# Two small DMAs issued by ScalarE instead of SyncE, and two more Relu blocks by halves

## The chip, the cores and the metric

The kernel runs on one core of a Trainium2 chip. The metric is device time in microseconds (us) of one execution, as the median of several runs. A lower number is better.

The core's engines each work through their own list of instructions in order and wait for each other on counting semaphores: TensorE (PE) multiplies matrices, VectorE (DVE) and ScalarE (ACT) do elementwise work and read PSUM, GpSimd (POOL) does elementwise work in SBUF, and SyncE (SP) issues most DMAs. Any of ACT, POOL and SP can issue a DMA; the transfer itself then runs on the core's 16 DMA engines.

## What is computed

A causal depthwise convolution of 7 taps over 4096 tokens, for 8 sequences of 192 channels, whose taps are the softmax of a weight for each of 8 heads. On its result, a feed-forward layer with 1536 hidden channels:

```python
w = exp(weight - max) ; w = w / (sum + 1e-09)          # 8 heads x 7 taps
x = einsum('hk,bskhg->bshg', w, x_unfolded)            # 8 x 4096 x 192
gate = maximum(x @ w_gate, 0.0)                        # 32768 x 1536
val  = x @ w_val
out  = (gate * val) @ w_out                            # 32768 x 192
```

## The kernel before

The tokens are worked in 16 units. A unit is 1024 tokens of one sequence and the same 1024 tokens of the sequence four further on; these two are the two **streams** (`st` 0 and 1). One stream lies on partitions 0 to 63 and the other on 64 to 127, and the 192 channels are three groups (`c` 0, 1, 2, "thirds") of 64. So the convolved input of unit 0 is the tile `xc[0]`, of 128 partitions, three thirds and 1024 tokens. A unit has two windows (`w`) of 512 tokens.

`gate_val(u, w)` makes the hidden layer of one window in 12 blocks (`f` 0 to 11, "first" to "twelfth") of 128 hidden channels. For one block PE runs six matmuls for gate and six for val (L600). ACT takes the Relu of gate from PSUM into `gr` (L611), and DVE multiplies it with val into `hT` (L612). Gate and val of a block have a PSUM buffer each, of four in turn, so the gate of block f+2 can't be begun before the Relu of block f is over, and its val not before DVE's product of block f. In four blocks of the first window (first, second, fifth, sixth) Relu and product are made by streams: two halves of 128x512, so that DVE can begin when the first half is there. The others are one instruction of 128x1024 each.

The start is arranged by hand. Unit 0's first 512 tokens are convolved by PE (`first_block`), and the window begins. The second 512 tokens are convolved by PE before the fifth block (`second_block`). Part of its result comes out on other partitions than it belongs: it is evicted to `held` (in the tile `out_s`, L433) and brought to its place by eight DMAs from SBUF to SBUF (L438): 40 partitions of the first third, 8 and 8 of the second, 40 of the last, each for both streams. SP issues all eight. The second window, `gate_val(0, 1)`, reads them: its first six gate matmuls go through the thirds in order, both streams each.

Behind the moves, SP issues nine DMA transposes (L885), which bring the input of unit 1 into channel layout (`x_r` from `x_p`). They need POOL's copies into `x_p` (L517). Ahead of the moves SP issues ten DMAs of a few hundred bytes that spread the taps (L854).

The DMAs of SP and ACT count on **eight semaphores, DMAHW0 to DMAHW7**. Each DMA adds 16 to one of them when it has landed, and before it is issued the issuing engine waits until the DMA that used that semaphore before has landed. The framework that builds the program hands them out in turn, one after the other, in the order in which its own plan of the program places the DMAs, over both engines together.

Beyond unit 0 everything repeats: 24 blocks of gate and val, then the projection with `Wo`, with the convolution of the units to come on ACT, DVE and POOL beside it.

Of the kernel before, what the change touches and what calls it, by code (L numbers as in the profile page):

```python
# [18 lines left out]
def kernel(  # L19
# [12 lines left out]
    nc = tc.nc  # L32
# [81 lines left out]
    def stage(p0, rows, st, n_st, jj, n):  # L114
        at = room[p0 : p0 + rows, 0, 0, 0:1]
        dims = [[D * GSUB, n_st], [D, n], [1, D]]
        return bass.AP(
            tensor=at.tensor,
            offset=at.offset + D * (GSUB * st + jj),
            ap=[at.ap[0]] + [d for d in dims if d[1] > 1],  # L120
        )
# [3 lines left out]
    def body(st):  # L125
# [8 lines left out]
        out=stage(PAD, FIRST, 0, 2, 0, 1),  # L134
        in_=bass.AP(
            tensor=x.tensor, offset=x.offset, ap=[[D, FIRST], [NB * S * D, 2], [1, D]]
        ),
# [111 lines left out]
    def bits(src, n, down, keep):  # L249
# [13 lines left out]
        out=mx[:], in_=wr[:], axis=mybir.AxisListType.X, op=ALU.max, negate=True  # L263
# [6 lines left out]
    with nc.allow_low_precision("zero and one"):  # L270
        nc.vector.tensor_tensor(
            out=same[:], in0=col[:, 0:SEG], in1=s_of[:].to_broadcast([SUB, SEG]), op=ALU.is_equal
# [12 lines left out]
    with nc.allow_low_precision("zero and one"):  # L285
        nc.vector.tensor_scalar(
            out=places[:, SUB - SEG : SUB - SEG + NROW],
# [7 lines left out]
        out=spread[0:SUB, 0, 0:H],  # L295
# [7 lines left out]
    with nc.allow_low_precision("products with one and zero"):  # L303
        nc.vector.tensor_tensor(
            out=diag[:],
# [6 lines left out]
    for a in range(2):  # L312
        for b in range(NSEG):
            nc.tensor.matmul(
                out=(bps, spread)[a][:, a, HB * SEG * b : HB * SEG * (b + 1)],
# [9 lines left out]
    for c in range(NCH):  # L325
        cols = slice(64 * c, 64 * c + 64)
        nc.scalar.copy(
            out=xts[0][0:ROWS0, 1:GSUB, 0, cols],
            in_=stage(0, ROWS0, 0, 1, 1, GSUB - 1)[:, :, cols],
# [28 lines left out]
    xc = {}  # L358
# [40 lines left out]
    def conv_heads(g, ps, bank, slots):  # L399


        xt = xts[g]
        toks = GROUPS[g][1]
        t0 = toks[0]
        ends = toks[1:] + [t0 + WIN]
        for jj in range(GSUB):
            col, n = toks[jj] - t0, ends[jj] - toks[jj]
            rows = n + PAD
            for i, (st, ch, h) in enumerate(slots):
                nc.tensor.matmul(  # L410
                    out=ps[32 * i : 32 * i + 32, bank, col : col + n],
                    lhsT=xt[0:rows, jj, st, ch : ch + 32],
                    rhs=band(h)[0:rows, 0:n],
                    start=True,
                    stop=True,
                    tile_position=(0, 32 * i),
                    skip_group_check=True,
                )
# [3 lines left out]
    def second_block():  # L422
        aside, inplace = [psum.tile([128, 2, 512], FP, name="ps") for _ in range(2)]
        conv_heads(1, aside, 0, [(0, ch, h) for ch, h in ASIDE])
        conv_heads(1, inplace, 0, [(st, ch, h) for st in range(2) for ch, h in ((0, 0), (160, 7))])
        conv_heads(1, inplace, 1, [(st, ch, h) for st in range(2) for ch, h in ((64, 3), (96, 4))])
        conv_heads(1, aside, 1, [(1, ch, h) for ch, h in ASIDE])
        late = slice(WIN, 2 * WIN)
        os_ = opool.tile([128, 4, D], FP, name="out_s")
        flat = os_[:].rearrange("p a d -> p (a d)").bitcast(F16)  # L430
        held = flat[:, 0 : 2 * WIN].rearrange("p (s t) -> p s t", s=2)
        nc.scalar.copy(out=xc[0][:, 0, late], in_=inplace[:, 0, :])
        nc.scalar.copy(out=held, in_=aside[:])  # L433
        nc.vector.tensor_copy(out=xc[0][:, 1, late], in_=inplace[:, 1, :])
        nc.vector.tensor_copy(out=xc[0][:, 2, late], in_=inplace[:, 0, :])
        for c, r, p0, n in ((0, 24, 8, 40), (1, 0, 48, 8), (1, 56, 72, 8), (2, 0, 80, 40)):
            for st in range(2):
                nc.sync.dma_start(  # L438
                    out=xc[0][64 * st + r : 64 * st + r + n, c, late],
                    in_=held[p0 : p0 + n, st, :],  # L440
                )

    HEADS = (((0, 1), (3, 4)), ((6, 7), (2, 5)))

# [140 lines left out]
    def gate_val(u, w):  # L585
        h = hpool.tile([128, NFF, 2, WIN], F16, name="hT")
        xcb = xc[u]
        for f in range(NFF):
            if u == 0 and w == 0 and f == 4:
                second_block()  # L590
            pss = [psum.tile([128, 2, 512], FP, name="ps") for _ in range(2)]
            order = [(i, c) for i in range(2) for c in range(NCH)]
            if u == 0 and w == 0 and f == 0:
                order = [(i, c) for c in range(NCH) for i in range(2)]
            M = 64 if 0 < u < NUNIT - 1 else 128
            for i, c in order:
                W = (Wg, Wv)[i]
                for st in range(2):
                    for m in range(0, 128, M):
                        nc.tensor.matmul(  # L600
                            out=pss[i][m : m + M, st, :],
                            lhsT=W[64 * st : 64 * st + 64, c, 128 * f + m : 128 * f + m + M],
                            rhs=xcb[64 * st : 64 * st + 64, c, WIN * w : WIN * (w + 1)],
                            start=(c == 0),
                            stop=(c == NCH - 1),
                            tile_position=(64 * st, m),
                        )
            by_stream = u == 0 and w == 0 and f in (0, 1, 4, 5)
            for sts in (slice(0, 1), slice(1, 2)) if by_stream else (slice(0, 2),):
                gr = gpool.tile([128, 2, WIN], F16, name="gr")  # L610
                nc.scalar.activation(out=gr[:, sts], in_=pss[0][:, sts], func=ACTF.Relu)  # L611
                nc.vector.tensor_tensor(  # L612
                    out=h[:, f, sts], in0=gr[:, sts], in1=pss[1][:, sts], op=ALU.mult
                )
        return h

    def slots():
# [232 lines left out]
    for h in range(H):  # L850
        r = G * h
        while r < G * (h + 1):
            c, n = r // 64, min(64 - r % 64, G * (h + 1) - r)
            nc.sync.dma_start(  # L854
                out=tap[r % 64 : r % 64 + n, c, :],
                in_=taps[h : h + 1, :].unsqueeze(1).to_broadcast([1, n, KW]),
# [18 lines left out]
    for u in range(NUNIT):  # L875
# [6 lines left out]
        if u == 0:  # L882
            hs.append(gate_val(0, 0))
            for go in turns:
                go()  # L885
# [23 lines left out]
        while len(hs) < 2:  # L909
            hs.append(gate_val(u, len(hs)))  # L910
# [50 lines left out]
```

## Time and profile before

| | us |
|---|---|
| median of 3 runs | 761.53 (761.35 to 761.76) |
| time of the profiled execution | 762.13 |
| its span in the trace | 760.4 |
| PE busy | 756.0 (99%) |
| DVE busy | 708.4 (93%) |
| ACT busy | 618.4 (81%) |
| POOL busy | 404.2 (53%) |

Times in the trace count from the start of the span. "SPq" and "ACTq" are the parts of SP and ACT that issue DMAs; the length of such a row is that of the issuing instruction, and the transfer lands later. In brackets at the end of a row stands how long the engine was idle before and what ended it. A page's shares are means over the whole span; this change touches a stretch of some 20 us at its start, so the rows of that stretch matter most.

### The profile page before, as it was taken

To read this page: it belongs to the slowest core of one execution; us is meant where nothing else is said; L and a number is where in the kernel's file an instruction comes from. 1 tells how busy PE (TensorE), PEld (TensorE's weight loads), DVE (VectorE), ACT (ScalarE), POOL (GpSimd) and SP (SyncE) were. 2 spreads that over 40 slices of the span, in tenths; PEclk is the share of its full clock that TensorE was granted. 3 is DMA by queue.
4 is the path that set the end of the run, shared out by engine and by line. 5 is a ranking of instruction groups with operands and counts; after the bars stand their busy time and mean duration, and the time that the engine had idled before them with its cause. 6 is when DMAs were issued, how large, how long until landed. Compare 5 with 4: busy or idle time off the path is not lost.

```text
span 760.4 us, 30579 instructions
## 1 busy us (share of the span) xinstructions
PE 756.0 (99%) x13597; PEld 484.5 (64%) x13597; DVE 708.4 (93%) x771; ACT 618.4 (81%) x725; POOL 404.2 (53%) x262
## 2 busy tenths in 40 slices
PE   9999999999999999999999999999999999999998
PEld 5595555555666666666666666666666666666548
DVE  7998999999999999999999999999999999999891
ACT  7787887978879798898988979788797887976672
POOL 9519549094490935819267291763908549091000
PEclk9999999999999999999999999999999999999999
DMA  9969229589396983949749597594966939544732
GB/s 135 129 106 134 24 64 176 140 98 195 91 183 151 87 184 98 206 119 119 171 93 180 134 147 172 80 183 112 173 145 101 178 109 139 158 113 110 187 85 84
DMA packets 231700, 100.61 MB, mean 132 GB/s; under 512 B 185296, under 2 KB 220816, under 8 KB 231568
## 3 DMA queue, kind: packets, MB, share of 16 engines
q1 hardware_dynamic: 190528, 83.12, 53.3%
q0 software_dynamic: 40896, 15.50, 19.9%
q8 instruction: 106, 1.74, 1.0%
q14 instruction: 26, 0.21, 0.1%
q10 hardware_dynamic: 144, 0.03, 0.0%
HBM read 31.48 MB, written 47.19 MB: 103 GB/s over the span
## 4 chain that ended last, share of the span: by engine, by line
PE 96%; DMA 2%; SPq 1%; ACT 0%; issue 0%; POOLq 0%
PE ps L600 63%; PE ps L713 29%; PE ps L629 3%; PE ps L680 1%; DMA tap<-taps 1%; SPq L854 1%; DMA xc<-out_s 1%; DMA x_h<-in_x_dram 1%; SPq L438 0%; ACT xc L397 0%; PE ps L456 0%; PE ps L379 0%; ACT acc L688 0%; ACT taps L848 0%; POOLq L945 0%
## 5 line engine op out<-in xcount | busy, mean ns | idle before, releaser
L612 DVE TENSOR_TENSOR hT<-gr,ps 128x1024 f16<-128x1024 f16 (+1 forms) x388 | 469.1, 1210 | 29.9 <-ACT gr L611 3.4
L611 ACT ACTIVATE gr<-ps 128x1024 f16<-128x1024 f32 (+1 forms) x388 | 393.3, 1015 | 100.8 <-PE ps L600 100.7
L548 POOL TENSOR_TENSOR prods<-prods 128x1344 f32<-128x1344 f32 x70 | 213.0, 3042 | 268.8 <-DVE prods L544 265.5
L600 PE MATMUL ps<-xc,Wg 64*64 64x512 f16 (+1 forms) x4320 | 322.6, 376 | 0.5 <-DMA xc<-out_s 0.5
L600 PE MATMUL ps<-xc,Wv 64*64 64x512 f16 (+1 forms) x4320 | 322.2, 376 | 0.0
L713 PE MATMUL ps<-hT,Wo 64*64 64x512 f16 x4032 | 220.2, 376 | 0.0
L600 PEld LDWEIGHTS <-Wg 64*64 64x64 f16 (+1 forms) x4320 | 155.4, 106 | 93.6 <-issue 0.6
L600 PEld LDWEIGHTS <-Wv 64*64 64x64 f16 (+1 forms) x4320 | 153.0, 105 | 96.3 <-issue 1.8
L713 PEld LDWEIGHTS <-Wo 64*64 64x64 f16 x4032 | 139.7, 107 | 77.8
L572 DVE SCALAR_TENSOR_TENSOR acc<-x_r,tap,acc 128x576 f32<-128x576 f16 x225 | 165.3, 813 | 0.0
L542 ACT ACTIVATE prods<-x_r,tap 128x448 f32<-128x448 f16 x222 | 127.2, 659 | 0.0
L735 ACT COPY x_h<-ps 128x2048 uint16<-128x2048 uint16 x28 | 51.8, 1848 | 8.8 <-PE ps L713 8.8
L215 POOL DMA_DIRECT2D x_e<-in_x_dram x58 | 46.9, 818 | 12.8 <-ACT acc L558 12.5
L517 POOL COPY x_p<-x_e 128x960 f16<-128x960 f16 (+1 forms) x58 | 50.4, 914 | 1.0 <-DMA x_e<-in_x_dram 0.9
L548 POOL TENSOR_TENSOR xc<-prods 128x1344 f16<-128x1344 f32 x14 | 42.5, 3038 | 1.1
L735 POOL COPY y<-x_h 128x2048 uint16<-128x2048 uint16 x14 | 26.6, 1898 | 23.3 <-ACT x_h L791 23.3
L572 DVE SCALAR_TENSOR_TENSOR xc<-x_r,tap,acc 128x576 f16<-128x576 f16 x45 | 34.1, 813 | 0.0
L558 ACT ACTIVATE acc<-x_r,tap 128x576 f32<-128x576 f16 x45 | 31.4, 765 | 0.0
L544 DVE TENSOR_SCALAR prods<-x_r,tap 128x448 f32<-128x448 f16 x70 | 27.7, 449 | 0.0
L629 PE MATMUL ps<-Wo,hT 64*128 64x192 f16 x576 | 24.6, 243 | 0.0
L629 PEld LDWEIGHTS <-hT 64*128 64x128 f16 x576 | 24.0, 94 | 0.4
L791 ACT COPY x_h<-ps 128x512 f32<-128x512 f32 x14 | 8.2, 587 | 10.9 <-ACT x_h L735 6.3
(69 smaller groups left out, 92.4 us busy)
## 6 DMA issues: line engine op xcount, KB each, us to landing
out_dram<-out_s SPq DMA_DIRECT2D x62, 384.0 KB
held<-x_h SPq DMA_DIRECT2D x14, 512.0 KB
held<-x_h SPq DMA_DIRECT2D x28, 256.0 KB
held<-y SPq DMA_DIRECT2D x14, 512.0 KB
x_e<-in_x_dram POOLq DMA_DIRECT2D x34, 192.0 KB, 6.7
x_e<-in_x_dram POOLq DMA_DIRECT2D x24, 240.0 KB, 5.3
x_r<-x_p SPq DMA_TRANSPOSE x131
out_s<-held SPq DMA_TRANSPOSE x56
```

What stands on the lines that cost most here:

```text
L215: first = nc.gpsimd.dma_start(out=xe[:, j0 + start : j0 + n, st, :, :].rearrange("p j c r -> p j (c r)"), in_=bass.AP(tensor=x.tensor, off ...
L517: nc.gpsimd.tensor_copy(out=xp[:, j0 : j0 + n, :, st, :], in_=xe[:, j0 : j0 + n, st, :, :])
L542: engine.activation(out=out, in_=in_, func=ACTF.Copy, scale=scale)
L548: nc.gpsimd.tensor_tensor(out=pr[:, 0] if k < KW - 1 else xc[v + 1][:, :, LDVE:UNIT], in0=pr[:, 0], in1=pr[:, k], op=ALU.add,)
L558: nc.scalar.activation(out=accs[v][:, c, :], in_=shifted(v, c, 0, 0), func=ACTF.Copy, scale=tap[:, c, 0:1],)
L572: nc.vector.scalar_tensor_tensor(out=xc[v][:, c, 0:LDVE] if k == KW - 1 else acc[:, c, :], in0=shifted(v, c, k, 0), scalar=tap[:, c, k : k ...
L600: nc.tensor.matmul(out=pss[i][m : m + M, st, :], lhsT=W[64 * st : 64 * st + 64, c, 128 * f + m : 128 * f + m + M], rhs=xcb[64 * st : 64 * ...
L611: nc.scalar.activation(out=gr[:, sts], in_=pss[0][:, sts], func=ACTF.Relu)
L612: nc.vector.tensor_tensor(out=h[:, f, sts], in0=gr[:, sts], in1=pss[1][:, sts], op=ALU.mult)
L629: mm = nc.tensor.matmul(out=outs[q], lhsT=h[64 * r : 64 * r + 64, f, st, 128 * q : 128 * (q + 1)], rhs=Wo[64 * r : 64 * r + 64, f, :], sta ...
L713: mm = nc.tensor.matmul(out=ps[bank][64 * half : 64 * half + 64], lhsT=Wo[64 * r : 64 * r + 64, f, d : d + 64], rhs=hs[w][64 * r : 64 * r ...
L735: copy(out=pt[:], in_=src[:].bitcast(U16).rearrange("p b (t l) -> p b l t", l=2))
```

## The change

The two moves of the last third (40 partitions, 512 tokens, one for each stream) are taken from SP's list. ACT issues them: the one for stream 0 behind the Relu of the sixth block (`f == 5`), that for stream 1 behind the Relu of the eighth (`f == 7`). The seventh and the ninth block (`f` 6 and 8), which follow them on ACT, are made by streams. Bytes, places and the other six moves stay.

```diff
-        for c, r, p0, n in ((0, 24, 8, 40), (1, 0, 48, 8), (1, 56, 72, 8), (2, 0, 80, 40)):
+
+        def move(queue, st, c, r, p0, n):
+            queue.dma_start(
+                out=xc[0][64 * st + r : 64 * st + r + n, c, late],
+                in_=held[p0 : p0 + n, st, :],
+            )
+
+        for piece in ((0, 24, 8, 40), (1, 0, 48, 8), (1, 56, 72, 8)):
             for st in range(2):
-                nc.sync.dma_start(
-                    out=xc[0][64 * st + r : 64 * st + r + n, c, late],
-                    in_=held[p0 : p0 + n, st, :],
-                )
+                move(nc.sync, st, *piece)
+        return [partial(move, nc.scalar, st, 2, 0, 80, 40) for st in range(2)]
@@ gate_val
             if u == 0 and w == 0 and f == 4:
-                second_block()
+                moves = second_block()
...
-            by_stream = u == 0 and w == 0 and f in (0, 1, 4, 5)
+            by_stream = u == 0 and w == 0 and f in (0, 1, 4, 5, 6, 8)
...
+            if u == 0 and w == 0 and f in (5, 7):
+                moves.pop(0)()
```

In the program that is built, this is ACT's order from the evictions of the second block on, before (`gr` is the Relu's output; the last number is the tile's shape; in brackets the semaphores that are waited for):

```order
L432 CAST xc<-ps 128x512 [waits PE_49]
L433 CAST out_s<-ps 128x1024 [waits PE_49]
L611 ACTIVATE gr<-ps 128x512 [waits DVE_49,PE_49]
L611 ACTIVATE gr<-ps 128x512 [waits DVE_49]
L611 ACTIVATE gr<-ps 128x512 [waits DVE_49,PE_49]
L611 ACTIVATE gr<-ps 128x512 [waits DVE_49]
L611 ACTIVATE gr<-ps 128x1024 [waits DVE_49,PE_49] x18
```

and with the change:

```order
L616 ACTIVATE gr<-ps 128x512 [waits DVE_49,PE_49]
L616 ACTIVATE gr<-ps 128x512 [waits DVE_49]
L438 DMA xc<-out_s 40x512 [waits DMAHW6_49]
L616 ACTIVATE gr<-ps 128x512 [waits DVE_49,PE_49]
L616 ACTIVATE gr<-ps 128x512 [waits DVE_49]
L616 ACTIVATE gr<-ps 128x1024 [waits DVE_49,PE_49]
L438 DMA xc<-out_s 40x512 [waits DMAHW5_49]
L616 ACTIVATE gr<-ps 128x512 [waits DVE_49,PE_49]
L616 ACTIVATE gr<-ps 128x512 [waits DVE_49]
L616 ACTIVATE gr<-ps 128x1024 [waits DVE_49,PE_49] x15
```

Two DMA issues now stand between Relus, and each waits for a DMA semaphore, DMAHW6 and DMAHW5.

On SP the same stretch, from the first move on, was before:

```order
L438 DMA xc<-out_s 40x512 [waits DMAHW5_49,Activation_49]
L438 DMA xc<-out_s 40x512 [waits DMAHW6_49]
L438 DMA xc<-out_s 8x512 [waits DMAHW7_49,DVE_49]
L438 DMA xc<-out_s 8x512 [waits DMAHW0_49]
L438 DMA xc<-out_s 8x512 [waits DMAHW1_49]
L438 DMA xc<-out_s 8x512 [waits DMAHW2_49]
L438 DMA xc<-out_s 40x512 [waits DMAHW3_49,DVE_49]
L438 DMA xc<-out_s 40x512 [waits DMAHW4_49]
L885 DMA_TRANSPOSE x_r<-x_p 128x3x128 [waits DMAHW5_49,Pool_49]
L885 DMA_TRANSPOSE x_r<-x_p 128x3x128 [waits DMAHW6_49]
L885 DMA_TRANSPOSE x_r<-x_p 128x3x128 [waits DMAHW7_49]
```

and with the change, from the last of the six moves that are left:

```order
L438 DMA xc<-out_s 8x512 [waits DMAHW2_49]
L892 DMA_TRANSPOSE x_r<-x_p 128x3x128 [waits DMAHW3_49,Pool_49]
L892 DMA_TRANSPOSE x_r<-x_p 128x3x128 [waits DMAHW4_49]
L892 DMA_TRANSPOSE x_r<-x_p 128x3x128 [waits DMAHW5_49]
L892 DMA_TRANSPOSE x_r<-x_p 128x3x128 [waits DMAHW7_49]
L892 DMA_TRANSPOSE x_r<-x_p 128x3x128 [waits DMAHW0_49]
L892 DMA_TRANSPOSE x_r<-x_p 128x3x128 [waits DMAHW1_49,Pool_49]
L892 DMA_TRANSPOSE x_r<-x_p 128x3x128 [waits DMAHW2_49]
L892 DMA_TRANSPOSE x_r<-x_p 128x3x128 [waits DMAHW3_49]
L892 DMA_TRANSPOSE x_r<-x_p 128x3x128 [waits DMAHW4_49]
L663 DMA out_dram<-out_s 128x4x192 [waits PE_49,DMAHW6_49,Activation_49]
```

The semaphores run on in turn, but with two gaps: DMAHW6 between the third and the fourth transpose, and DMAHW5 between the ninth and the first output. These two went to ACT's moves. The counts in the built program say the same: ACT's first move waits until DMAHW6 stands at 32 (a tap DMA and the move of the first third for stream 1), its second until DMAHW5 stands at 48 (a tap DMA, the move of the first third for stream 0, and the third transpose).

## The prediction

> **What bounds the kernel now.** I read the page first, for the engine that sets the end:
>
> ```profile
> span 760.4 us, 30579 instructions
> PE 756.0 (99%) x13597; PEld 484.5 (64%) x13597; DVE 708.4 (93%) x771; ACT 618.4 (81%) x725; POOL 404.2 (53%) x262
> PE 96%; DMA 2%; SPq 1%; ACT 0%; issue 0%; POOLq 0%
> ```
>
> PE is busy for 99% of the span and makes 96% of the chain that ended last. Whatever makes PE wait is paid in full, since nothing later has slack to give it back; whatever spares PE a wait is earned in full. So only PE's waits in the stretch of the change count. The chain in order of time and PE's timeline there:
>
> ```profile
> 20.89 4.88 DMA xc<-out_s
> 25.81 4.19 PE ps L600 x36
> ...
> 21.95 0.83 PE L600 MATMUL ps<-xc,Wg 64*128 64x512 f16 x6
> 22.60 0.83 PE L600 MATMUL ps<-xc,Wv 64*128 64x512 f16 x6
> 23.25 0.83 PE L600 MATMUL ps<-xc,Wg 64*128 64x512 f16 x6
> 23.90 0.83 PE L600 MATMUL ps<-xc,Wv 64*128 64x512 f16 x6
> 24.54 0.81 PE L600 MATMUL ps<-xc,Wg 64*128 64x512 f16 x5
> 25.81 0.37 PE L600 MATMUL ps<-xc,Wg 64*128 64x512 f16 x1 [0.46 <-DMA xc<-out_s]
> ```
>
> Six matmuls start every 0.648 us (24.54 − 21.95 is four times that). The sixth of the second window's first gate should start 0.43 us after 24.54, with its pair, at 24.97; it starts at 25.81. It waited 0.84 us for the last of SP's eight moves, issued at 20.89 and landed at 25.77. This is what there is to win: 0.84 us, 0.11% of the span.
>
> **What is removed and moved.** SP gives up two issues of 0.7 us; behind them on SP stand only the transposes, which wait for POOL's copies until 24.1, so that saves nothing. If ACT's copy of the last move were issued right behind the eighth Relu, at about 20.2, it would land by 25.1 (the same 4.88 us), and 0.7 us of the 0.84 would be won. Whether it can be issued then is the question.
>
> **The waits that come with it.** Both moves now stand in ACT's own list, between Relus, and each waits for a DMA semaphore. Behind the first stand the Relus from the seventh block on, behind the second those from the ninth on; DVE's products wait for the Relus, and PE for both, two blocks later.
>
> The first waits until SP's second move (first third, stream 1) has landed. Its issue row, and the one tap DMA whose landing the chain shows:
>
> ```profile
> 16.25 0.73 SPq L438 DMA_DIRECT2D xc<-out_s  x1
> ...
> 13.10 6.27 DMA tap<-taps
> ...
> Wv<-in_moe_w_val_dram POOLq DMA_DIRECT2D x1, 48.0 KB, 3.4
> ```
>
> With the 4.88 us of the last move it lands at about 21.1; the 6.27 of the tap would make it 22.5, and the shortest landing of this stretch, 3.4 of a load of like size, 19.7. ACT has been ready since 17.43:
>
> ```profile
> 15.32 2.11 ACT L611 ACTIVATE gr<-ps 128x512 f16<-128x512 f32 x4
> 17.64 1.02 ACT L611 ACTIVATE gr<-ps 128x1024 f16<-128x1024 f32 x1 [0.21 <-PE ps L600]
> 18.93 1.02 ACT L611 ACTIVATE gr<-ps 128x1024 f16<-128x1024 f32 x1 [0.27 <-PE ps L600]
> 20.23 1.02 ACT L611 ACTIVATE gr<-ps 128x1024 f16<-128x1024 f32 x1 [0.27 <-PE ps L600]
> ```
>
> So the seventh Relu slips from 17.64 to about 21.6, and PE, out of buffers after the eighth block's val at 19.36, stands about 3.3 us (to 21.1 + 0.5 for the issue + two half Relus of 0.53). With the old wait gone this alone would be a net loss of 1.5 to 4 us.
>
> The second waits until DMAHW5 stands at 48: a tap, SP's first move, and **the third transpose**, which SP issues only after POOL's copies. SP's queue there:
>
> ```profile
> 24.15 1.31 SPq L885 DMA_TRANSPOSE x_r<-x_p  x1
> 25.52 1.65 SPq L885 DMA_TRANSPOSE x_r<-x_p  x1
> 27.20 1.87 SPq L885 DMA_TRANSPOSE x_r<-x_p  x1
> ```
>
> Its issue ends at 29.07. Nothing in the change makes it earlier: the first transpose starts when POOL has ended its second copy, POOL waits for nobody on ACT or PE there, and SP was idle before it:
>
> ```profile
> 22.21 1.91 POOL L517 COPY x_p<-x_e 128x960 f16<-128x960 f16 x2
> 24.07 1.02 POOL L869 DMA_DIRECT2D Wo<-in_moe_w_out_dram  x1
> 28.21 1.50 POOL L97 DMA_DIRECT2D x_h<-in_x_dram  x2 [0.32 <-issue]
> ```
>
> When does it land? No row gives a transpose's landing, but the DMA view gives what SP's queue (q1) moved, here from 24.15 to 33, to 34.8 and to 39.2:
>
> ```profile
> q1 hardware_dynamic: 1061, 0.26, 54.6%
> ...
> q1 hardware_dynamic: 1356, 0.33, 50.3%
> ...
> q1 hardware_dynamic: 3723, 0.89, 70.1%
> Wo<-in_moe_w_out_dram POOLq DMA_DIRECT2D x1, 576.0 KB, 9.2
> x_h<-in_x_dram POOLq DMA_DIRECT2D x2, 192.0 KB, 9.5
> ```
>
> 0.89 MB is nine transposes, so three are 0.30 MB. They are through not before some 33.7 (on the line from 0.26 MB at 33 to 0.33 MB at 34.8), and that only if the fourth and fifth, issued by then, have not yet moved a byte. The queue crawls because POOL's 576 KB of `Wo`, issued at 24.07, take 9.2 us of the same engines, to 33.3, and the `x_h` loads follow. I take 34.7, with 33.7 and 36 as ends. Until then ACT stands, and the ninth Relu is held back from 20.23 to behind it.
>
> **What it costs PE.** PE needs the ninth Relu's buffer for the eleventh block's gate, which began at 21.95. Now:
>
> 34.7, when the third transpose lands. Plus ACT's issue: ACT's one DMA in this trace took 0.37, SP's moves around 0.73:
>
> ```profile
> 757.91 0.37 ACTq L691 DMA_DIRECT2D out_dram<-acc  x1
> ```
>
> I take 0.5, as POOL issues nothing at that time. Plus the two halves of the ninth Relu, 2 × 0.53 (2.11 for four). That gives 36.3 for the eleventh gate instead of 21.95: **+14.3**. PE has stood for some 10 us by then, since the tenth block, the last for which it had buffers, is over by about 26.
>
> Then PE's speed after the stand. The nearest rows are its start, also after idling, and the 0.84 us wait, after which it went on at the old rate:
>
> ```profile
> 0.78 3.04 PE L161 MATMUL ps<-const-bfloat16-1.0 128*128 128x512 bf16 x7 [0.78 <-PEq L945]
> 3.96 0.61 PE L161 MATMUL ps<-const-bfloat16-1.0 128*128 128x512 bf16 x1
> 4.85 0.49 PE L161 MATMUL ps<-const-bfloat16-1.0 128*128 128x512 bf16 x2
> ```
>
> At the start seven matmuls of 512 columns took 3.04 us, 0.43 each, where the pair of L600 takes 0.216; at 3.96 a single one still took 0.61, against 0.37 at 25.81; at 4.85 two took 0.49 together. So for 3.8 us from its first matmul PE ran at half rate. (The granted clock of that stretch is given as 1.00 all the same.) An idle stretch of 10 us is nearer to that start than to 0.84 us: I take half rate for 3.8 us, **+1.9**. At the other end, full rate, a smaller loss stands in its place: DVE's product of the ninth block, two halves of 0.62 behind the two Relu halves, ends at 37.0, and PE would wait for it 0.3 us between gate and val of the eleventh block:
>
> ```profile
> 15.97 2.48 DVE L612 TENSOR_TENSOR hT<-gr,ps 128x512 f16<-128x512 f16 x4
> ```
>
> At half rate the gate itself lasts to 37.6, and DVE is hidden. The Trainium skill (TensorE: Matmul & The Clock Gate, Part 1) says that PE falls back to half clock after an idle window of about 3.4 us and needs about 3.4 us of sustained work to leave it; by its figure the term would be an estimated +1.7, and its cold gap for 512 columns, 427 ns, agrees with the 0.43 here.
>
> Less the old wait: the second move, issued at 34.7, lands at 39.6 (4.88) to 41.0 (6.27); PE needs it at 36.3 + 1.9 + 3.0 = 41.2 (four half blocks of 0.648 and 0.43). So that wait is gone: **−0.84**.
>
> Sum: 14.3 + 1.9 − 0.84 = **+15.4 us**. The seventh and ninth block by streams change little: four halves take DVE 2.48 and ACT 2.11 against 2.44 and 2.04 for two whole ones, beside ACT's stand. All that comes behind, transposes, loads and unit 1, was ready before it was needed and is so more than ever; PE does not catch up at 99%. On the profiled execution's span that is 775.8; on the median of the runs, which lies 1.1 above that span, 761.53 + 15.4 = **776.9**.
>
> **The rivals.**
> - PE keeps its full rate over the stand: 14.3 + 0.3 − 0.84 = +13.8, 775.3. For it: the granted clock shows no dip anywhere. Against it: the start.
> - The third transpose lands later than 36, or ACT's issue takes 0.75 and the move lands late: +17 to +19, about 779.5. For it: the packets of later transposes share the queue. Against it: the rest of the traffic is the same as before.
> - The second move is not held, because its semaphore's third count comes from something earlier than the transpose. Then only the first wait stays: ACT stands to 21.1, PE loses the 3.3 and 0.3 to DVE behind it, and wins 0.84: +2.8, 764.3. Against it: the gap in SP's semaphores right behind the ninth transpose, and the count of 48.
> - The other side: the change does what its words say. Both semaphores are free when ACT comes to them, before 17.4 and before 20.2, the moves land by 25.1, and the wait at 25.81 shrinks by 0.7, with each issue (0.37 to 0.73) mostly in ACT's gaps of 0.21 and 0.27 between Relus: 760.8. It decides from the point at which the second move is issued before 20.9. Against it: SP's second move can't have landed at 17.43, 1.2 us after its issue began, when no landing of this stretch took under 3.4.
>
> **How the numbers follow.** Forecast 0.76; full rate 0.11; later landing 0.05; only the first wait 0.04; as the words say 0.04. The ends of the terms give 760.4's run 774.2 (33.7, issue 0.37, full rate) to 778.5 (36, issue 0.75, half rate); some room for the later landing makes the range 773.8 to 779.3. It holds the first two cases and part of the third and leaves out about 0.13. A measurement can't tell less than 0.2% (1.5 us) from no change: faster by more has only half of the last rival's neighbourhood, 0.01; within it the rest of that rival and a small part of the one before, 0.05; slower 0.94.
>
> **What would show it.** In the changed kernel's timeline, ACT's first move (L438 on ACTq) should stand some 2 to 5 us behind the sixth Relu, the second at 34 to 36, right after the third transpose lands; PE should show two stands in the first window, about 2 to 4 us before the ninth block and about 10 before the eleventh, both ended by ACT's `gr`; the eleventh block's matmuls should come 0.43 apart for about 3.8 us; and the wait at the second window's first gate should be gone. From there on the rows should be those of before, 15 us later. I am wrong if ACT's second move starts before 30, or if PE's stand before the eleventh block is under 8 us.

## The result and the profile after

| | before | changed |
|---|---|---|
| median of 5 runs each, us | 761.70 (761.35 to 762.18) | 781.09 (779.20 to 781.84) |
| ratio, 95% interval | | 1.0249 [1.0232, 1.0265] |
| time of the profiled execution | 762.13 | 779.62 |
| its span | 760.4 | 777.8 |

The change costs 19.4 us in the medians and 17.5 in the two profiled executions (17.4 in their spans). The forecast was 776.9, with a range that ended at 779.3: the sign and the place were right, the size too small by 4.2 us.

The page of the changed kernel, its parts 1 and 5:

```profile
span 777.8 us, 30579 instructions
PE 760.2 (98%) x13597; PEld 478.2 (61%) x13597; DVE 708.5 (91%) x773; ACT 618.3 (79%) x727; POOL 404.1 (52%) x262
L605 PE MATMUL ps<-xc,Wg 64*64 64x512 f16 (+1 forms) x4320 | 323.0, 377 | 13.9 <-ACT gr L616 13.9
```

PE does the same 13597 matmuls in 4.2 us more of busy time, and has 13.9 us of idle time ahead of the gate matmuls that all go to ACT's `gr`. Together that is 18.1, of which 0.84 us of the old wait is given back. Rows picked from the timeline of the changed kernel show both at their places (start, length, engine, line, and in brackets the idle time before):

```profile
20.17 1.33 ACTq L438 DMA_DIRECT2D xc<-out_s  x1
21.60 2.00 ACT L616 ACTIVATE gr<-ps 128x512 f16<-128x512 f32 x3 [4.12 <-DMA xc<-out_s]
22.74 1.46 PE L605 MATMUL ps<-xc,Wg 64*128 64x512 f16 x6 [3.14 <-ACT gr L616]
...
35.79 0.72 ACTq L438 DMA_DIRECT2D xc<-out_s  x1
36.62 2.00 ACT L616 ACTIVATE gr<-ps 128x512 f16<-128x512 f32 x3 [13.01 <-DMA x_r<-x_p]
37.76 1.47 PE L605 MATMUL ps<-xc,Wg 64*128 64x512 f16 x6 [10.74 <-ACT gr L616]
38.99 1.51 PE L605 MATMUL ps<-xc,Wv 64*128 64x512 f16 x6
40.27 1.51 PE L605 MATMUL ps<-xc,Wg 64*128 64x512 f16 x6
41.55 1.50 PE L605 MATMUL ps<-xc,Wv 64*128 64x512 f16 x6
42.83 0.87 PE L605 MATMUL ps<-xc,Wg 64*128 64x512 f16 x6
```

ACT's first move is issued at 20.17 and the Relu behind it has waited 4.12 us, put down to a move of SP; its second goes out at 35.79, and the Relu behind it has waited 13.01 us for a transpose. PE stands 3.14 us before the ninth block and 10.74 before the eleventh. Then six matmuls start every 1.28 us, twice the old 0.648, up to 42.83, where the second window's first gate begins with no wait.

The windows view cuts the same stretch where the granted clock, the share of its full clock that PE was given, changes (columns: stretch, us, busy time and instructions of PE, PEld, DVE, ACT, POOL, granted clock, DMA share, GB/s):

```profile
19.02:22.43 3.41, 0.58 (x6) 0.18 (x3) 0.20 (x1) 0.83 (x2) 3.37 (x5) 1.00 0.98 122
22.43:25.84 3.41, 3.10 (x16) 1.31 (x17) 2.31 (x3) 1.18 (x2) 3.41 (x4) 0.50 1.04 115
25.84:29.26 3.42, 1.18 (x12) 0.43 (x8) 0.00 (x0) 0.00 (x0) 2.85 (x9) 1.00 1.17 140
29.26:42.91 13.65, 5.16 (x26) 2.12 (x27) 3.73 (x4) 4.05 (x5) 0.00 (x0) 0.50 1.15 105
42.91:46.32 3.41, 3.41 (x34) 1.74 (x32) 2.68 (x3) 2.05 (x2) 0.00 (x0) 1.00 0.00 0
```

The clock is halved for one stretch of 3.41 us after the first stand and for four of them (13.65) during and after the second. In the second, PE works from 37.76 on, so it loses half of the 5.15 us up to 42.91.

The chain of waits from 24 to 45 us names the releaser (start, us, what):

```profile
27.25 8.52 DMA x_r<-x_p
...
35.79 0.72 ACTq L438
```

The third transpose's issue began at 27.25, and the chain gives it 8.52 us to land, at 35.77; ACT's move follows at once.

### The profile page after: what moved, and what is told of

The parts are those of the page before. It is cut to its first block, busy times and chain, and to the rows that moved or that the text cites. A ratio compares the mean times of both kernels' runs of the same rounds, so it can differ in the third digit from the quotient of the medians.

```text
span 777.8 us, 30579 instructions
## 1 busy us (share of the span) xinstructions
PE 760.2 (98%) x13597; PEld 478.2 (61%) x13597; DVE 708.5 (91%) x773; ACT 618.3 (79%) x727; POOL 404.1 (52%) x262
## 4 chain that ended last, share of the span: by engine, by line
PE 95%; POOL 2%; DMA 2%; SPq 0%; issue 0%; ACT 0%; ACTq 0%; POOLq 0%
PE ps L605 63%; PE ps L720 28%; PE ps L636 3%; DMA x_r<-x_p 1%; PE ps L687 1%; DMA Wv<-in_moe_w_val_dram 1%; POOL x_e L215 0%; POOL Wg L177 0%; SPq L892 0%; POOL Wg L184 0%; POOL Wv L177 0%; POOL Wv L184 0%; POOL x_p L522 0%; POOL Wv L193 0%; POOL x_h L139 0%
## 5 line engine op out<-in xcount | busy, mean ns | idle before, releaser
L605 PE MATMUL ps<-xc,Wg 64*64 64x512 f16 (+1 forms) x4320 | 323.0, 377 | 13.9 <-ACT gr L616 13.9
L605 PEld LDWEIGHTS <-Wg 64*64 64x64 f16 (+1 forms) x4320 | 152.4, 106 | 112.8 <-issue 17.6
L720 PEld LDWEIGHTS <-Wo 64*64 64x64 f16 x4032 | 137.3, 107 | 80.3
L549 DVE TENSOR_SCALAR prods<-x_r,tap 128x448 f32<-128x448 f16 x70 | 27.6, 447 | 0.0
```

The source lines that it names most:

```text
L605: nc.tensor.matmul(out=pss[i][m : m + M, st, :], lhsT=W[64 * st : 64 * st + 64, c, 128 * f + m : 128 * f + m + M], rhs=xcb[64 * st : 64 * ...
L720: mm = nc.tensor.matmul(out=ps[bank][64 * half : 64 * half + 64], lhsT=Wo[64 * r : 64 * r + 64, f, d : d + 64], rhs=hs[w][64 * r : 64 * r ...
```

## The experiments

Each kernel is the changed one with the edit shown, if nothing else is said. Each time stands against runs of the kernel before that were taken beside it.

**One equation for them.** From the eleventh block on nothing differs between these kernels but what PE loses there. So a span should be the start of the eleventh block's gate, plus half of what PE then works at half clock, plus the wait at the second window's first gate, plus a rest that is always the same. From the profiles, in us:

| kernel | eleventh gate | half clock until | wait, 2nd window | sum | span | rest |
|---|---|---|---|---|---|---|
| before | 21.95 | none | 0.84 | 22.8 | 760.4 | 737.6 |
| first_only | 27.64 | over by then | 0 | 27.6 | 765.2 | 737.6 |
| quiet_queue | 31.96 | 37.77 | 0 | 34.9 | 772.4 | 737.5 |
| wo_late | 35.37 | 38.13 | 0.82 | 37.6 | 775.1 | 737.5 |
| second_only | 36.34 | 41.05 | 0 | 38.7 | 776.2 | 737.5 |
| xh_late | 35.71 | 41.44 | 0 | 38.6 | 776.6 | 738.0 |
| after_again | 38.51 | 41.61 | 0 | 40.1 | 777.6 | 737.5 |
| changed, first profile | 37.76 | 42.91 | 0 | 40.3 | 777.8 | 737.5 |

Over 17 us of difference the rest stays within 0.5, and within 0.1 in all but one. kept_warm fits as well (its rest is 737.6). kept_warm_longer has 738.5: its last matmul ends 3.6 us before the end of the span, where the others have 2.7, so 0.9 us of it is lost at the kernel's end, and why isn't known. That is the frame for what follows: what holds the eleventh gate back, what sets its time, and how long the half clock lasts. The kernels are named in the sections below.

**free_semaphores: both moves on ACT, but behind semaphores that are free.** The first transpose is made to wait for the ninth Relu. The plan then places ACT's moves ahead of all transposes and hands them DMAHW3 and DMAHW4, whose users before them are the ninth and tenth tap DMA.

```diff
...
-            for go in turns:
-                go()
+            for n, go in enumerate(turns):
+                step = go()
+                if n == 0:
+                    tc.add_manual_dep(step.ins, relus[8].ins.name, SYNC, ...)
```

> The changed kernel, but the first of the nine transposes is also made to wait for the ninth Relu (over before 24 us, when POOL's copies release it anyway). With that the framework's plan places both ACT moves ahead of the transposes, and they get DMAHW3 and DMAHW4, whose users before are the ninth and tenth tap DMA, landed by about 18. Theory (the loss is the wait on semaphores that belong to SP's second move and to the third transpose): ACT's moves start at about 17.8 and 20.6, cost 0.7 to 1.3 us each, PE stands under 1 us in the first window, and the time is 761.0 to 762.5. Rival (issuing from ACT, or the move behind a Relu, is the cost by itself): 775 or more.

762.96 (762.16 to 763.63, 10 runs) against 762.00 (761.31 to 762.76, 19 runs): ratio 1.0013 [1.0003, 1.0022]. Its timeline:

```profile
17.28 1.33 ACTq L438 DMA_DIRECT2D xc<-out_s  x1
...
19.98 1.02 ACT L617 ACTIVATE gr<-ps 128x1024 f16<-128x1024 f32 x1 [0.17 <-PE ps L606]
19.98 0.72 ACTq L438 DMA_DIRECT2D xc<-out_s  x1
```

The moves go out at 17.28 and 19.98, beside Relus, and no stand is left. The time is 0.5 us above the range that was expected. All but 1 us of the loss is gone although ACT issues the same two moves between the same Relus, and the transposes start later than in the changed kernel (25.99 against 24.24). So it isn't issuing from ACT that costs, it is the semaphore that the plan hands to the move. Where its remaining 1 us goes isn't settled: its profiled execution, with a span of 760.9, shows waits for the first weights' halves (1.8 us in four waits of the weight loads for POOL's copies in L184) of which the kernel before shows 0.3, and only one execution was profiled.

**streams_only: the two more blocks by halves, all moves on SP.** The kernel before with one line of the change:

```diff
-            by_stream = u == 0 and w == 0 and f in (0, 1, 4, 5)
+            by_stream = u == 0 and w == 0 and f in (0, 1, 4, 5, 6, 8)
```

> The kernel before, with the seventh and ninth block by streams and all eight moves still on SP. Theory: the halves cost nothing, 761.4 to 762.0, and PE still waits 0.8 us at the second window's first gate. Rival (the halves hold DVE or ACT up): 762.5 or more, with a stand of PE behind the ninth block.

762.07 (761.32 to 762.71, 10 runs), ratio 1.0000 [0.9991, 1.0010]. The blocks by halves cost nothing that can be measured, as forecast. One thing missed: in its profiled execution (span 759.5) the wait at the second window's first gate isn't there:

```profile
23.88 0.83 PE L600 MATMUL ps<-xc,Wv 64*128 64x512 f16 x6
24.52 0.83 PE L600 MATMUL ps<-xc,Wg 64*128 64x512 f16 x6
25.17 0.83 PE L600 MATMUL ps<-xc,Wv 64*128 64x512 f16 x6
```

All eight moves are still SP's, and reorder below has no wait there either, so the 0.84 us that the prediction called all there is to win seem to be a matter of the execution. The kernel before has it in a profile of 762.13, its median is 761.5, and its lowest runs are at 761.25.

**first_only and second_only: one move on ACT, the other back on SP.**

```diff
# first_only
-        return [partial(move, nc.scalar, st, 2, 0, 80, 40) for st in range(2)]
+        move(nc.sync, 1, 2, 0, 80, 40)
+        return [partial(move, nc.scalar, 0, 2, 0, 80, 40)]
-            if u == 0 and w == 0 and f in (5, 7):
+            if u == 0 and w == 0 and f == 5:
# second_only
+        move(nc.sync, 0, 2, 0, 80, 40)
+        return [partial(move, nc.scalar, 1, 2, 0, 80, 40)]
+            if u == 0 and w == 0 and f == 7:
```

> Of the two moves only that of stream 0 goes to ACT, behind the sixth Relu; that of stream 1 stays on SP as its last. The ACT move waits for SP's second move, as in the changed kernel, and nothing on ACT waits for a transpose. Theory: ACT stands from 17.4 to about 20.2, PE for 3.1 to 3.5 us before the ninth block, half rate from then costs up to 1.7, the wait at the second window's gate is hidden behind it: 764.3 to 767. Rival (one stand gives the other, or the second move is the whole loss): 762.5 or less.

> Of the two moves only that of stream 1 goes to ACT, behind the eighth Relu; that of stream 0 stays on SP as its last. DMAHW5 now waits for a tap, SP's first move and the second transpose (one transpose earlier than in the changed kernel). Theory (the stands don't add: the longer one hides the shorter): no stand before the ninth block, one before the eleventh that ends about 1.5 us earlier than in the changed kernel, with the second transpose's landing at about 34.3; 777 to 779.5. Rival (the first stand adds its 5 us to the second): 773 to 775.

first_only: 766.90 (766.07 to 767.03, 4 runs) against 761.55, ratio 1.0065 [1.0050, 1.0080]. second_only: 778.35 (776.60 to 779.23, 4 runs) against 761.32, ratio 1.0220 [1.0206, 1.0234]. The timelines, first_only:

```profile
20.81 1.32 ACTq L438 DMA_DIRECT2D xc<-out_s  x1
23.37 1.35 PE L606 MATMUL ps<-xc,Wg 64*128 64x512 f16 x6 [3.18 <-ACT gr L617]
24.48 1.52 PE L606 MATMUL ps<-xc,Wv 64*128 64x512 f16 x6
25.76 1.42 PE L606 MATMUL ps<-xc,Wg 64*128 64x512 f16 x6
26.99 0.83 PE L606 MATMUL ps<-xc,Wv 64*128 64x512 f16 x6
27.64 0.83 PE L606 MATMUL ps<-xc,Wg 64*128 64x512 f16 x6
```

and second_only:

```profile
33.78 1.32 ACTq L438 DMA_DIRECT2D xc<-out_s  x1
36.34 1.46 PE L606 MATMUL ps<-xc,Wg 64*128 64x512 f16 x6 [14.16 <-ACT gr L617]
```

Alone, the moves cost 5.4 and 17.0 us, both within the ranges that were expected, and together 17.9 (after_again) to 19.4: the stands don't add. Each is a time before which ACT can't go on, and the later one covers the earlier. first_only also prices what the prediction's rival "only the first wait" left out. A stand of 3.18 us is followed by half clock too: the gate and val of the ninth and the gate of the tenth block take 3.62 us, from 23.37 to 26.99, where full rate takes 1.94, which is 1.7 of the 2.6 by which that rival's 764.3 was too low. In second_only the count that ACT waits for is reached with the second transpose, since one move fewer is ACT's.

**wo_late, xh_late, quiet_queue: fewer other bytes beside the transposes.** wo_late issues the 576 KB of `Wo` behind the `x_h` loads. xh_late leaves `Wo` where it is and holds the `x_h` loads until the ninth Relu. quiet_queue holds both until then.

```diff
# quiet_queue; xh_late holds load_x(2) alone, wo_late only puts Wo behind load_x(2)
...
-    nc.gpsimd.dma_start(out=Wo[:], ...)
-    load_rest(load_x(2))
...
             for go in turns:
                 go()
+            wo = nc.gpsimd.dma_start(out=Wo[:], ...)
+            tc.add_manual_dep(wo.ins, relus[8].ins.name, SYNC, ...)
+            load_rest(load_x(2))
```

> The changed kernel, with POOL's load of Wo issued behind the x_h loads, not ahead of POOL's second pair of copies. Theory (the third transpose lands late because Wo's 576 KB are ahead of it on the same engines): it lands at 30 to 32.5 and not at 35.8, ACT's second move starts then, and the time falls by 3 to 5.5 us against the changed kernel, to 775.5 to 778. Rival (transposes take this long by themselves): the second move starts at 34.5 or later, 780 to 782.

> The changed kernel, with only POOL's two loads of x_h (192 KB each) held back until the ninth Relu; Wo stays where it is. With both loads held back the third transpose landed at 30.0, with Wo moved behind x_h at 33.4, and in the changed kernel, where x_h is issued 0.9 us earlier than in the kernel before, at 35.8 to 36.6. Theory (each load in front costs its share, and the earlier x_h is what made the landing later than the 34.7 of the kernel before): it lands at 32.5 to 34.3, 776 to 778. Rival (x_h comes too late to matter; Wo alone does it): 35.3 or later, 779 or more.

> The changed kernel, with POOL's loads of Wo and x_h held back until the ninth Relu, so that from 24 us on the transposes have the DMA engines to themselves (Wo and x_h are not needed before the second window is over). Theory (the third transpose lands 35.8 and not at about 30 because both loads share the engines): ACT's second move starts at 29.5 to 31.5, PE's stand before the eleventh block shrinks to about 5 us, 772.5 to 775.5. Rival (a transpose takes 7 to 8 us from issue to landing by itself, as with Wo moved alone, where it still landed at 33.4): the second move starts at 33 or later, 775 or more.

wo_late: 775.72 (774.91 to 776.90, 4 runs) against 762.00, ratio 1.0179 [1.0164, 1.0194]. xh_late: 778.13 (777.88 to 778.41, 4 runs) against 761.32, ratio 1.0219 [1.0203, 1.0234]. quiet_queue: 773.15 (772.67 to 774.15, 4 runs) against 761.55, ratio 1.0147 [1.0130, 1.0164]. ACT's second move and PE's second stand, in wo_late:

```profile
33.41 0.72 ACTq L438 DMA_DIRECT2D xc<-out_s  x1
35.37 1.46 PE L605 MATMUL ps<-xc,Wg 64*128 64x512 f16 x6 [8.12 <-ACT gr L616]
40.57 0.37 PE L605 MATMUL ps<-xc,Wg 64*128 64x512 f16 x1 [0.44 <-DMA xc<-out_s]
```

in xh_late:

```profile
33.75 0.72 ACTq L441 DMA_DIRECT2D xc<-out_s  x1
35.71 1.46 PE L609 MATMUL ps<-xc,Wg 64*128 64x512 f16 x6 [10.55 <-ACT gr L620]
```

and in quiet_queue:

```profile
30.00 0.72 ACTq L438 DMA_DIRECT2D xc<-out_s  x1
31.96 1.46 PE L606 MATMUL ps<-xc,Wg 64*128 64x512 f16 x6 [4.89 <-ACT gr L617]
```

The move goes out at 35.79 (36.55 in after_again) with both loads beside the transposes, 33.4 to 33.8 with one put later, 30.00 with neither. So ACT's wait ends with a transpose, and POOL's loads set when. The transposes' issues start alike in all of them (23.68 to 24.68); with neither load beside them three take 5.7 us from there, beside both 11.5 to 12.2. In wo_late the old wait for a move is back, 0.82 us: by the chain the move, issued at 33.41 behind the `Wo` load of 28.73, took 7.12 us to land. In xh_late the gate starts 2.05 us earlier than in the first profile of the changed kernel, and the span gains only 1.2. Of the difference, 0.3 is the half clock, which falls on 5.73 us of work instead of 5.15; the other 0.5 is in the rest (738.0) and lies behind 75 us, with a cause that is open. For wo_late the expectation's landing missed (33.4) and its time held, since the half clock was short there (2.76 us). In xh_late the landing was as expected and the median 0.1 above the range; in quiet_queue both held.

**after_again: the changed kernel once more, beside the next.**

> The changed kernel once more, profiled and timed beside the next three. Theory (its runs spread over 2.6 us because the landing of the third transpose and the place of the half-rate stretch move): its profile differs from the first one in these two places and agrees elsewhere; 779 to 782.

779.43 (779.05 to 780.93, 4 runs) against 761.55 (761.27 to 762.40, 7 runs), ratio 1.0236 [1.0220, 1.0251]. Timeline and windows:

```profile
36.55 0.72 ACTq L438 DMA_DIRECT2D xc<-out_s  x1
38.51 1.47 PE L605 MATMUL ps<-xc,Wg 64*128 64x512 f16 x6 [12.61 <-ACT gr L616]
...
42.61 0.82 PE L605 MATMUL ps<-xc,Wg 64*128 64x512 f16 x6
```

```profile
24.54:27.95 3.41, 1.36 (x14) 0.51 (x9) 0.48 (x1) 0.00 (x0) 3.03 (x5) 1.00 0.80 96
27.95:41.61 13.66, 3.10 (x16) 1.32 (x17) 2.76 (x4) 3.02 (x4) 1.27 (x6) 0.50 1.27 124
```

The same program lands its transpose 0.76 us later and loses no time by it, because the half clock ends at 41.61 instead of 42.91. PE comes 10.6 us into the 13.66 here, and 8.5 us into the 13.65 in the first profile. How much of the half clock falls on work is a matter of where the stand's end lies on these stretches, and that differs from one execution to the next.

**kept_warm and kept_warm_longer: PE given work to do in its stands.** 14 and 44 (in the second kernel 14 and 54) further matmuls of 512 columns with zero weights behind the val of the eighth and the tenth block. They add zeros to finished sums; the values are the same.

```diff
...
+    FILL = {7: 14, 9: 44}
...
+            fill = FILL.get(f, 0) if u == 0 and w == 0 else 0
+            for n in range(fill):
+                nc.tensor.matmul(
+                    out=pss[1][:, n % 2, :],
+                    lhsT=nought[:],
+                    rhs=xcb[:, 0, 0:WIN],
...
```

> The changed kernel, with 14 matmuls of zero weights (128x512) added to the eighth block's val and 44 to the tenth's, which add nothing to the sums: PE works through most of both stands. Theory (PE falls to half rate in the stands and pays 2.6 us for it from the eleventh block on): the clock stays at 1.00, the matmuls of the eleventh block start 0.216 apart, and the time falls by 2 to 2.6 us, to 778 to 779.2, with a narrower spread of the runs. Rival (the half rate costs nothing, since DVE's products set the pace there): 780.5 to 781.5 with the clock at 1.00.

> As kept_warm, with 54 added matmuls for 44, so that PE works to within 1 us of the ninth Relu and no idle stretch of some 3 us is left before the eleventh block. Theory (the half rate costs 2 to 3 us): clock 1.00 in every run, no matmul 0.43 behind the one before, 776.3 to 778.3, 2.5 to 4 below the changed kernel of the same call. Rival (DVE's products set the pace behind the stand, so that the half rate is hidden): within 1 us of the changed kernel.

kept_warm: 779.45 (776.58 to 780.71, 4 runs) against 762.00, ratio 1.0222 [1.0199, 1.0244]. Its added matmuls ended at 35.5, the transpose came late, PE stood 3.24 us more, and the clock was halved after all, so the expected clock and time were both missed. That one decides nothing, so the next has ten more. kept_warm_longer: 778.26 (778.23 to 778.97, 4 runs) against 761.55, ratio 1.0219 [1.0204, 1.0234]. Its timeline:

```profile
26.00 11.83 PE L618 MATMUL ps<-xc,nought 128*128 128x512 f16 x54
36.56 0.73 ACTq L440 DMA_DIRECT2D xc<-out_s  x1
38.53 0.82 PE L608 MATMUL ps<-xc,Wg 64*128 64x512 f16 x6 [0.70 <-ACT gr L628]
39.37 0.82 PE L608 MATMUL ps<-xc,Wv 64*128 64x512 f16 x6
...
41.35 0.83 PE L608 MATMUL ps<-xc,Wg 64*128 64x512 f16 x6
```

With the move at the same time as in after_again (36.56, 36.55) and the gate too (38.53, 38.51), the eleventh and twelfth block take 2.82 us instead of 4.10, and the granted clock over them is 1.00. So the doubled pitch is the clock after idling and not something in the operands or the queue. It is worth 1.3 us there, and 2.25 against the first profile (5.07). The prediction's smaller loss at full rate is there too: gate to val takes 0.84 instead of 0.648, a wait of 0.19 for DVE where it had 0.3. In the medians it is 1.2 us against after_again, less than the 2.5 to 4 expected; the intervals of the two ratios overlap, so this size rests on the rows of the two blocks. The spans differ by only 0.4, as this execution loses 0.9 us behind its last matmul.

**reorder: a try at the 0.84 us without ACT.** The kernel before, with SP's moves of the last third put ahead of the four small ones:

```diff
-        for c, r, p0, n in ((0, 24, 8, 40), (1, 0, 48, 8), (1, 56, 72, 8), (2, 0, 80, 40)):
+        for c, r, p0, n in ((0, 24, 8, 40), (2, 0, 80, 40), (1, 0, 48, 8), (1, 56, 72, 8)):
```

> The kernel before, all eight moves on SP, but the two of the last third (40 partitions) go ahead of the four of the second third (8 partitions each), so that a small one is issued last, at about 20.9. Theory (the wait at the second window's gate is for a 40 KB transfer issued last; small ones landed 3.4 to 4 us after their issue): PE's wait at the sixth matmul is gone or under 0.2, 761.0 to 761.6, 0.2 to 0.9 below the kernel before. Rival (the wait is only there in some executions, as the profile of the halves alone showed none, and the time of an execution is set by when the first weights land): same within 0.3 us.

761.53 (761.28 to 761.82, 11 runs) against 761.32 (761.25 to 762.07, 15 runs), ratio 1.0001 [0.9992, 1.0010]. So the rival came, the same time within 0.3 us. The profile shows no wait at the gate, but most runs of the kernel before beside it were at 761.25 to 761.5 as well, 0.6 to 0.9 under the profiled execution that shows the wait: in most executions there seems to be nothing to win. No trace gives the 3.4 to 4 us that the expectation takes for the small moves; 3.4 is the row of a 48 KB load, and 3.89 is what the chain of first_only gives a move of 40 partitions. None of these kernels beats the one before.

## Why the prediction was right in its reasons and wrong in its size

**Right.** That each of ACT's moves waits for the DMA that used its semaphore before, SP's second move and the third transpose, that the Relus queue behind it, and that PE runs out of buffers two blocks later. The signs came as listed: first move at 20.17 (2 to 5 us behind the sixth Relu), second at 35.79 (34 to 36), stands of 3.14 and 10.74 us (3.3 and about 10), matmuls 0.43 apart behind the second, no wait at the second window, and PE never catching up. free_semaphores shows that the semaphore is the cause, as it changes that and keeps the issue on ACT.

**Wrong: the term of +14.3, in the transpose's landing.** The eleventh gate came 15.8 us later than before (37.76 against 21.95). Most of the missing 1.5 is the landing: the prediction took 34.7, and it was 35.77, in after_again 36.53. The prediction read it from the bytes of SP's queue in the kernel before: three transposes are 0.30 MB, so the third was taken as landed about 1 us after that much was through. (On the line that it drew, 0.30 MB falls at 34.0 and not at 33.7; the trace has it at 33.2.) The DMA view of the changed kernel from 24.24 us to the landing at 35.77 shows how far the queue had come by then:

```profile
q1 hardware_dynamic: 1731, 0.41, 22.6%
```

and that of the kernel before from 24.15 to 35.8:

```profile
q1 hardware_dynamic: 1645, 0.40, 50.5%
```

When the third transpose landed, over four transposes' worth of bytes were through, in after_again five (0.50 MB). So the fourth and fifth moved their bytes beside the third, which the prediction named as a condition and allowed 1 us for. At 35.8 the kernel before had moved about as much, and by 36.5 it had moved 0.52 MB: read with these marks, its own trace gives a landing at about 35.8 to 36.5. No trace shows the landing in the kernel before itself, so this is an estimate. Nor is there one right mark: at the landing 0.30 MB were through in quiet_queue, 0.31 in wo_late and 0.53 in xh_late. The bytes of a queue with other transfers behind leave the landing of one of them open by more than the ends of 33.7 and 36 that were taken.

The other ground, that "the rest of the traffic is the same as before", isn't quite so either. POOL's second pair of copies and the `x_h` loads behind them start 0.87 us earlier. The timeline of POOL and the DMA view from 20 to 32 us, before:

```profile
26.03 1.60 POOL L517 COPY x_p<-x_e 128x768 f16<-128x768 f16 x2 [0.94 <-DMA x_e<-in_x_dram]
x_e<-in_x_dram POOLq DMA_DIRECT2D x2, 192.0 KB, 5.3
```

and with the change:

```profile
25.17 1.60 POOL L522 COPY x_p<-x_e 128x768 f16<-128x768 f16 x2
27.34 1.49 POOL L97 DMA_DIRECT2D x_h<-in_x_dram  x2 [0.32 <-issue]
x_e<-in_x_dram POOLq DMA_DIRECT2D x2, 192.0 KB, 4.2
```

The loads of `x_e` land sooner, and the copies no longer wait for them. It may be that the last of the eight moves, no longer in the engines at 20.9, made room; but first_only, which issues its last two moves at 20.51 and 20.81, has the early `x_h` too (3.10 us behind the first transpose, as here; 4.06 in the kernel before), so that cause isn't shown. With the earlier `x_h` SP's queue falls behind for a while: 0.29 MB are through at 34.4, which the kernel before had passed by 33.2. By 35.8 the two are about level. What the 0.87 us adds to the landing wasn't tried alone. That POOL's loads as such set the landing is shown by wo_late, xh_late and quiet_queue.

**The same term, in ACT's issue and the Relu.** From the landing to the gate were taken 0.5 + 2 × 0.53 = 1.6 us; it was 1.99 (35.77 to 37.76). ACT's issue took 0.72, with 0.1 to the Relu behind it. The 0.37 of the output at the kernel's end, which pulled the estimate down, was another kind of transfer; SP's rows of such moves, 0.73, were the near ones and would have been right. POOL issued nothing at 35.79, and it took 0.72 all the same.

**The term of +1.9.** Half rate held for 5.15 us, not 3.8: 2.6 us. The start's 3.8 us was taken for a duration. The profiles show that it isn't one: after the second stand it was 2.76, 3.10, 4.71, 5.15, 5.73 and 5.81 us in six of them, each ending at the edge of a stretch of 3.41. Full rate, at 0.11 a rival, fell with the 0.50 in the windows. The prediction has no half clock behind the first stand, for which it took the 0.3 of DVE. It was there for 3.41 us, but the second stand covers it here; alone, in first_only, it costs 1.7.

These three differences are 1.07 + 0.39 + 0.68 = 2.1 us, which is the 2.0 between the forecast's span of 775.8 and the 777.8 measured.

**The rest, from span to median.** 4.2 us separate the medians. The prediction put its median 1.1 us above the span, because the profiled execution of before was 0.6 slower than its own median. The changed kernel's profiled execution is 1.8 above its span, and 1.5 below the median of its five runs. The nine runs of the changed kernel lie from 779.05 to 781.84, median 779.62: by those the forecast is 2.7 short. What made the runs at 781 to 782 slower is open, as none of them was profiled. Their mean granted clock is 0.989, that of the first profile with its five half-clock stretches (after_again has four and 0.991), so they can hardly have had more such stretches than it.

**The range** was put together from the ends of terms of one execution. It had no room for what differs between executions once a stand ends on a transfer in a full queue and on the edge of a clock stretch: 2.8 us over nine runs, where before varies by 1.5 over all its runs. The rival "later landing", 779.5, came nearest: the change cost 17.5 us in the profiled executions, where it has +17 to +19, and its ground, that packets of later transposes share the queue, is what the 0.41 MB show. Its landing beyond 36 came in after_again and was just missed in the first profile; its late move came in neither. It stood at 0.05 on the ground that the rest of the traffic is the same, which doesn't rule it out.

## What to carry to other kernels

A DMA moved to a compute engine's queue takes a semaphore out of a shared rotation with it: find the DMA that used that semaphore before, and when it lands, since the whole engine behind the issue waits for it. Don't take such a landing for the moment when a queue has moved the bytes up to it: here those behind it had moved up to 0.2 MB by then. Take ends that are wide enough for that, and for loads beside it that the change may shift. Once a matmul engine stands for some 3 us or more, add half of the half-clock time as a span of several us rather than a figure, and widen the range by it.

## What the runs showed of the hardware

- **The clock after a stand.** In every profile with a stand the granted clock changes on a grid of 3.41 us, and a stretch is at 0.50 after one in which PE did little: 0.58 us of work in 3.41 (19.02 to 22.43), 1.18 in 3.42 (25.84 to 29.26) and, in after_again, 1.36 in 3.41 (24.54 to 27.95) were each followed by half clock, 3.10 in 3.41 by full clock. So PE needn't be idle for a whole stretch. At full clock the edge lies between 1.50 us of work (wo_late, 21.10 to 24.52, followed by half clock) and 1.63 (second_only, 20.55 to 23.96, followed by full clock). So a stand of some 3 us may pass without a fall: that of 3.17 us in after_again lies across two stretches with 2.02 and 1.63 us of work, and the ninth block behind it ran at full clock. The Trainium skill (TensorE: Matmul & The Clock Gate, Part 1) gives a free-running window of 3413 ns; the trace agrees, in the 3.41. It puts the fall after an idle window, and these rows show it after windows that weren't idle.
- **ACT's first move takes 1.32 to 1.34 us to issue**, its second 0.72 or 0.73, in every kernel here with moves on ACT, whether the first waited (20.17) or not (17.28). In second_only, where the first is the other move, it is again the first that takes 1.32. Why isn't known; the kernel before has one small output as ACT's only DMA, and that took 0.37.
- **An issue on ACT doesn't hold up a Relu already ahead of it**: in free_semaphores the issue at 19.98 and a Relu of 1.02 us start together, and the next Relu isn't late. It costs time where the Relu behind it is due: at 35.79 in the changed kernel 0.83 us from issue to Relu, of the 13.01 that ACT stood.
